# Attention scores in native float32 in the two row halves of TensorE, in a fused attention and MLP kernel

## The chip, the cores and the metric

The kernel runs on one core of a Trainium2 chip, in one launch. The metric is the device time of that launch in microseconds (us); the number given for a kernel is the median of several executions. A profile is one execution recorded by the hardware profiler; its span goes from the first to the last instruction of the program.

## The reference, cut to what matters

```python
# batch 4, 12 heads, 448 positions, 64 numbers per head, all float32
def _attn_ref(q, k, v, w_pre, w_post):
    scores = scale * np.matmul(q, k.transpose(0, 1, 3, 2))
    scores = np.einsum('bhij,hg->bgij', scores, w_pre)      # heads are mixed
    scores = scores - np.max(scores, axis=-1, keepdims=True)
    attn = np.exp(scores)
    attn = attn / (np.sum(attn, axis=-1, keepdims=True) + 1e-09)
    attn = np.einsum('bhij,hg->bgij', attn, w_post)         # and mixed again
    return np.matmul(attn, v)

def _moe_ref(x, w1, w2, w3, w_out):
    return ((x @ w1) * (x @ w2) @ w3) @ w_out

def _moe2_ref(x, w_in, w_out):
    h = np.maximum(x @ w_in, 0.0)
    return h * h @ w_out
# reference = _moe2_ref(_moe_ref(heads of _attn_ref side by side))
```

The weights of the two MLPs arrive as 64-bit words and are narrowed to float32 on the chip. The product w3 @ w_out is formed once at the start and used in place of the two.

## The kernel before, in words

**Precision.** Most products are made of "fp32r" parts: a float32 operand is split into a high part (a rounded copy) and a low part (the rest), and a product is two or three matmuls over these parts. Two products of attention are in native float32 instead: the mixing of the heads before the softmax (`premix`, L380) and the product with v (`pv`, L478). A native float32 matmul stands in the trace as two weight loads and two matmuls.

**Stages.** The program has three. First the product w3 @ w_out (`Prod34`, L119 to L224), in two halves: weights are loaded, joined from their words by VectorE (L93, L95, L97), rounded to the high part by ScalarE (`high`, L111), and the low part is formed by GpSimd (`rest`, L115). In `half1` (L211) the first loop has eight pieces c of 12 matmuls each; ahead of each piece `stage` (L149) issues the preparation of later pieces, and behind it `between(c)` calls `prologue(8 + c)` (L796). Behind this loop stand four blocks of 24 matmuls. Then attention, in 16 chunks n of 120 or 88 query rows (four per batch). Then the two MLPs (`Moe`), about 830 us.

**A chunk of attention.** `scores` (L347) makes the 448 scores of one head for all rows of the chunk. Here a low part is carried along in the contraction: k lies twice, in partitions 0 to 63 and 64 to 127, once as its high and once as its low part (`high_k` L307, `low_k` L315), and q as high and low tiles (`high_q` L330, `low_q` L338); so one head is two fp32r matmuls over 128 partitions and 448 columns:

```python
for i, t in enumerate((self.qh[n, g4], self.ql[n, g4])):
    nc.tensor.matmul(
        sc[:ic], t[:, hh * ic : hh * ic + ic], self.kt[b, h // 2][:, h % 2], start=(i == 0), stop=(i == 1)
    )
```

The result lies in a PSUM tile `sc` of one bank, with two buffers. `evac` (L363) copies it to SBUF with ScalarE, one head at a time. When all 12 heads of a chunk are there, `regroup` (L368) moves blocks of 10 rows by 12 heads to 120 partitions by DMA, so that `premix` can mix heads. From there each block g goes through rowmax (VectorE, L386), `expo` (ScalarE, L394), the normalisation split into fp16 high and low parts (`p_hi` L419, `p_lo` L426), `tmix` (12 fp16 matmuls, L436) and its copy out of PSUM (`p2_evac`, L442: ScalarE where g is a multiple of 4, else VectorE). When a chunk is complete, `pv` multiplies by v. It works on two heads at a time, whose results go to partitions 0 to 63 and 64 to 127 of a PSUM tile, so each matmul uses 64 of TensorE's columns: two column halves.

**Order.** `attention_step(g)` (L549) issues one step for each of 180 blocks. `ORDER` (L536) sets what stands behind what on each engine: on TensorE `pv`, `premix`, `scores`, `tmix`; on ScalarE `evac` (of the step before), `p_hi`, `p2_act`, `pv_out`, `expo`. `LAG` says how many steps behind a block each part runs. `attention_plan` (L510) spreads the 12 heads of chunk n over the steps of the chunk before, and sets when q and k are loaded and split. The first chunk, n = 0, has its own list, `PRO` (L504): at which i of `prologue(i)` its loads, splits, scores and copies are issued, that is behind which piece of the w3 @ w_out product; i = 8 to 15 belong to the eight pieces of the first loop of `half1`, 16 to 19 to its four blocks. Every engine works through its own instructions in the order of issue.

Of the kernel before, what the change touches and what calls it, by code (L numbers as in the profile page):

```python
# [20 lines left out]
IC = 120  # L21
# [13 lines left out]
def fused_kernel(ctx, tc, q, k, v, w_pre, w_post, w1, w2, w3t, wo, win, wo2, eye, out):  # L35
# [83 lines left out]
    class Prod34:  # L119
# [61 lines left out]
        def half0(self, ps, between):  # L181
            acc = {(m, h): ps.tile([128, HC], F, name=f"p34_{m}_{h}") for m in range(4) for h in range(2)}
            for s in range(self.n0):
                self.stage(s)
                c, todo = self.seq[s][1], self.seq[s][5]
                for m, h in todo:
                    self.product(acc[m, h], m, h, (c,))
                if todo and todo[0][1]:
                    between(c)
            for m in range(4):  # L190
                if m > 1:
                    self.stage(self.n0 - 2 + m)
                o = f32(self.spare.tile([128, 2, S], R, tag="kt", name=f"o34_{m}", bufs=8))
                o = o.rearrange("p e j -> p (e j)")[:, :DM]
                nc.scalar.activation(o[:, :HC], acc[m, 0], AF.Copy)
                nc.vector.tensor_copy(o[:, HC:], acc[m, 1])
                nc.scalar.dma_start(
                    w34d[:, :, m].rearrange("n p c -> p n c"), o.rearrange("p (n c) -> p n c", c=128)
                )

        def store(self, m, h, acc):
            if m % 2 == 0:
                self.o = self.spare.tile([128, 3, 2, 128], F, tag="kraw", name=f"o34_{m}_{h}", bufs=2)
# [38 lines left out]
    class Attention:  # L242
        def __init__(self, const, ka, ps):
            self.const, self.ka, self.ps, self.sc = const, ka, ps, {}
            self.done = set()
            self.kt, self.kraw, self.qraw, self.qh, self.ql = {}, {}, {}, {}, {}
# [12 lines left out]


        def setup_load(self):
            nc.vector.memset(self.ones, 1.0)
            for x in self.phl:
                for t in x:
                    nc.vector.memset(t[:, S:], 0.0)
# [13 lines left out]
        def setup_post(self):  # L279
            kw, kab = (self.ka.tile([120, 12, 10], F, tag="qraw", name=x, bufs=2) for x in ("kw", "kab"))  # L280
# [17 lines left out]

        def load_k(self, b, r):
            if b == 0 and r in (2, 3):  # L300
                raw = f32(self.ka.tile([128, 2, S], R, tag="kt", name=f"kraw{b}_{r}", bufs=8))
            else:
                raw = self.ka.tile([128, 2, S], F, tag="kraw", name=f"kraw{b}_{r}", bufs=2)
            nc.sync.dma_start(raw, k[b, :, 2 * r : 2 * r + 2])
            self.kraw[b, r] = raw

        def high_k(self, b, r):  # L307
            t = self.ka.tile([128, 2, S], R, tag="kt", name=f"kt{b}_{r}", bufs=8)
            if b:
                nc.vector.tensor_copy(t, self.kraw[b, r])  # L310
            else:
                nc.scalar.activation(t, self.kraw[b, r], AF.Copy)
            self.kt[b, r] = t

        def low_k(self, b, r):  # L315
            raw, t = self.kraw.pop((b, r)), self.kt[b, r]
            for e in range(2):
                eng = nc.gpsimd if b else nc.vector
                eng.tensor_tensor(t[64:128, e], raw[64:128, e], f32(t[64:128, e]), ALU.subtract)  # L319
            self.done.add(("k", b, r))  # L320

        def load_q(self, n, g4):
            b, c = divmod(n, 4)
            i0, ic, _ = CHUNKS[c]
            o = 12 * i0 + 4 * g4 * ic
            raw = self.ka.tile([128, 4 * IC], F, tag="qraw", name=f"qraw{n}_{g4}", bufs=2)
            nc.sync.dma_start(raw[:, : 4 * ic], q[b, :, o : o + 4 * ic])
            self.qraw[n, g4] = raw[:, : 4 * ic]

        def high_q(self, n, g4):  # L330
            th = self.ka.tile([128, 4 * IC], R, tag="qh", name=f"qh{n}_{g4}", bufs=3)
            th = self.qh[n, g4] = th[:, : 4 * CHUNKS[n % 4][1]]
            if n:
                nc.vector.tensor_copy(th, self.qraw[n, g4])
            else:
                nc.scalar.activation(th, self.qraw[n, g4], AF.Copy)

        def low_q(self, n, g4):  # L338
            tl = self.ka.tile([128, 4 * IC], R, tag="ql", name=f"ql{n}_{g4}", bufs=3)
            tl = self.ql[n, g4] = tl[:, : 4 * CHUNKS[n % 4][1]]  # L340
            nc.gpsimd.tensor_tensor(tl, self.qraw.pop((n, g4)), f32(self.qh[n, g4]), ALU.subtract)

        def split_q(self, n, g4):
            self.high_q(n, g4)
            self.low_q(n, g4)

        def scores(self, n, h):  # L347
            b, c = divmod(n, 4)
            ic = CHUNKS[c][1]
            assert ("k", b, h // 2) in self.done  # L350
            if h == 0:
# [15 lines left out]

        def regroup(self, g):  # L368
            n, r, nr, o, cnt = blocks[g]
            assert all(("s", n, h) in self.done for h in range(NH))  # L370
# [83 lines left out]
        def p2_act(self, g):  # L454
            if g % 4 == 0:
                self.p2_evac(g, 0)

        def p2_dve(self, g):
            if g % 4:
# [34 lines left out]
    def spread(lo, hi, items):  # L494
# [3 lines left out]
    AT = {"sc": 1, "lq": 6, "hq": 3, "pv": 5, "k": -9, "ks": 4, "v": -6}  # L498
# [6 lines left out]
        "load_q": (2, 4, 9), "split_q": (5, 8, 13), "load_k": (7, 7, 8, 8, 8, 8), "high_k": (8, 9, 9, 12, 12, 12),  # L505
        "low_k": (9, 10, 12, 13, 13, 13), "scores": (10, 11, 12, 13, 15, 14), "evac": (10, 11, 13, 14, 15, 14),
# [3 lines left out]
    def attention_plan():  # L510
# [5 lines left out]
        for n in range(16):  # L516
            b = n // 4
            if n:
                for t, h in spread(first[n - 1] - RG + AT["sc"], first[n] - RG - 1, range(NH)):
                    add(t, "scores", n, h)  # L520
                    if h % 4 == 0:
                        add(t - AT["lq"], "load_q", n, h // 4)
                        add(t - AT["hq"], "high_q", n, h // 4)
            for t, x in spread(first[n + 1] + AT["pv"], first[n + 2] + AT["pv"], range(NH // 2)):
                add(t, "pv", n, x)
        for b in range(1, B):
            for r in range(NH // 2):
                t = first[4 * b - 2] + AT["k"] + AT["ks"] * r
                add(t - 3, "load_k", b, r)
                add(t, "high_k", b, r)  # L530
# [8 lines left out]
        ("rowmax", "p_lo", "high_q", "norm_recip", "p2_dve", "high_k"),  # L539
        ("norm_add", "low_q", "low_k"),  # L540
# [6 lines left out]
    AFTER = {"pv_out": "pv", "low_q": "high_q", "low_k": "high_k"}  # L547
# [238 lines left out]
    with tc.manual_schedule(), ExitStack() as base:  # L786
# [9 lines left out]
        def prologue(i):  # L796
# [5 lines left out]
            for kind in ("load_k", "load_q"):  # L802
                for x in at(kind):
                    getattr(A, kind)(0, x)
            for x in at("evac"):
                if PRO["scores"][x] < i:
                    A.evac(0, 2 * x)
                    A.evac(0, 2 * x + 1)
            for kind in ("low_k", "high_k", "split_q"):
                for x in at(kind):  # L810
                    getattr(A, kind)(0, x)
            for x in at("scores"):
                for h in (2 * x, 2 * x + 1):
                    A.scores(0, h)
                    if PRO["evac"][x] == i:
                        A.evac(0, h)
# [19 lines left out]
        for g in step:  # L836
            attention_step(A, g, ev)
            if g == closed:
# [3 lines left out]
                heads = (x for i in range(2) for x in M.early(  # L842
                    i, lambda i: ps.tile([128, TB], F, tag="sc", name=f"e{i}", bufs=2)
                ))
# [65 lines left out]
```

## Time and profile before

| | |
|---|---|
| time, median of 3 runs | 1403.97 us (1403.86 to 1404.88) |
| time of the profiled execution | 1406.93 us |
| its span, first to last instruction | 1405.1 us |
| TensorE (PE) busy | 1360.5 us, 97% of the span |
| VectorE (DVE), ScalarE (ACT), GpSimd (POOL) busy | 919.4, 714.0, 413.5 us |
| mean granted TensorE clock | 0.99 |

How to read it: the trace has one row per instruction. PE is the matmul side of TensorE, PEld its weight loads. A busy share is an average over stages with different limits, so it is read stage by stage. The ends of matmul rows are modelled, so neighbouring rows overlap; how long a group of matmuls holds the engine is better read from the chain of waits, in which each piece ends where the next begins.

### The profile page before, as it was taken

The page shows a single profiled execution, that of the slowest core. Times are in us where ns is not written, and L with a number is a line of the kernel's source. Part 1 is how long each engine was busy: PE and PEld are TensorE (multiplying, and loading weights), DVE is VectorE, ACT ScalarE, POOL GpSimd, SP SyncE. Part 2 cuts the span into 40 slices and gives each one's busy share as a digit, 9 for nine tenths or more (in the row PEclk, how much of TensorE's full clock was granted, in tenths as well). Part 3 has the DMA queues.
Part 4 walks back from the last instruction along what each step waited for, and adds up shares of the span by engine and source line. Part 5 has one row for each costly group of instructions (what it writes and reads, how often), then busy time and mean ns, then how long its engine had stood idle before and what let it go on. Part 6 is the DMA issues. An engine that isn't in the chain of part 4 may idle for free.

```text
span 1405.1 us, 24056 instructions
## 1 busy us (share of the span) xinstructions
PE 1360.5 (97%) x8858; PEld 1141.8 (81%) x8858; DVE 919.4 (65%) x1561; ACT 714.0 (51%) x1529; POOL 413.5 (29%) x424
## 2 busy tenths in 40 slices
PE   6779999999999998999999999999999999999998
PEld 5767666667667666899999999999999999999998
DVE  8963887886887779655217944985555128935962
ACT  4455887877777877434224533543343224533430
POOL 4531351351242113222222222233222222322231
PEclk9889999999999999999999999999999999999999
DMA  7754455454545335434123342455343123432341
GB/s 216 228 187 159 157 167 163 158 177 150 169 165 169 119 128 157 139 102 113 54 69 101 124 120 73 122 176 175 115 115 91 59 78 96 131 115 79 117 145 54
DMA packets 95514, 183.77 MB, mean 131 GB/s; under 512 B 20581, under 2 KB 62053, under 8 KB 94949
## 3 DMA queue, kind: packets, MB, share of 16 engines
q1 hardware_dynamic: 89861, 178.82, 41.2%
q10 hardware_dynamic: 5536, 3.42, 0.8%
q8 instruction: 70, 1.15, 0.4%
q14 instruction: 47, 0.39, 0.1%
HBM read 129.52 MB, written 14.16 MB: 102 GB/s over the span
## 4 chain that ended last, share of the span: by engine, by line
PE 89%; DVE 5%; ACT 2%; issue 2%; DMA 1%; POOL 1%; DVEq 0%; ACTq 0%; POOLq 0%
PE l L54 50%; PE sp L380 10%; PE y L54 8%; PE tp L436 7%; PE pv L478 6%; PE sc L358 5%; PE q L54 2%; DVE pl L426 1%; DVE f L93 1%; DVE f L95 1%; DVE f L97 1%; PE p L54 1%; DVE p L451 1%; PE e L54 1%; ACT ph L419 1%
## 5 line engine op out<-in xcount | busy, mean ns | idle before, releaser
L115 POOL TENSOR_TENSOR wl<-f,wh 128x384 fp32r<-128x384 f32 (+1 forms) x176 | 195.6, 1115 | 508.5 <-ACT wh L111 492.8
L93 DVE TENSOR_SCALAR f<-y 128x384 int32<-128x384 int32 (+2 forms) x209 | 146.9, 703 | 88.2 <-POOL wl L115 83.3
L426 DVE SCALAR_TENSOR_TENSOR pl<-p,sm,ph 120x448 f16<-120x448 f32 x180 | 138.9, 772 | 77.0 <-ACT ph L419 76.3
L380 PE MATMUL sp<-r,kpre 120*120 120x448 f32 x360 | 178.2, 577 | 1.2 <-ACT p L394 0.8
L436 PEld LDWEIGHTS <-ph 120*128 120x128 f16 (+1 forms) x1440 | 105.5, 98 | 52.6 <-issue 52.6
L97 DVE SCALAR_TENSOR_TENSOR f<-raw,f 128x384 int32<-128x384 int32 (+2 forms) x209 | 140.4, 672 | 6.1
L95 DVE SCALAR_TENSOR_TENSOR f<-y,f 128x384 int32<-128x384 int32 (+2 forms) x209 | 140.3, 672 | 6.1
L54 PE MATMUL l<-blh,wh 128*128 128x448 f32 x384 | 141.1, 368 | 0.0
L54 PE MATMUL l<-bhh,wl 128*128 128x448 f32 x384 | 141.1, 368 | 0.0
L54 PE MATMUL l<-bhh,wh 128*128 128x448 f32 x384 | 141.1, 368 | 0.0
L111 ACT ACTIVATE wh<-f 128x384 fp32r<-128x384 f32 (+1 forms) x176 | 96.5, 549 | 86.5 <-DVE f L97 80.9
L365 ACT ACTIVATE s<-sc 120x448 f32<-120x448 f32 (+1 forms) x192 | 99.2, 543 | 76.4 <-PE sc L358 73.0
L436 PE MATMUL tp<-kwh,ph 120*128 120x120 f16 x720 | 125.7, 219 | 1.1 <-DVE p L451 1.1
L394 ACT ACTIVATE p<-sp,nm 120x448 f32<-120x448 f32 x180 | 114.2, 635 | 23.4 <-DVE nm L386 21.9
L386 DVE TENSOR_REDUCE nm<-sp 120x1 f32<-120x448 f32 x180 | 110.6, 615 | 21.0 <-PE sp L380 19.8
L358 PE MATMUL sc<-kt,qh 128*120 128x448 f32 (+1 forms) x192 | 119.5, 622 | 5.0 <-DVE kt L319 4.6
L436 PE MATMUL tp<-kwh,pl 120*128 120x120 f16 x720 | 124.1, 216 | 0.0
L436 PE MATMUL tp<-kwl,ph 120*128 120x120 f16 x720 | 124.0, 216 | 0.0
L81 ACT ACTIVATE y<-raw 128x384 f32<-128x384 f32 (+2 forms) x209 | 120.6, 577 | 5.9 <-DMA raw<-w3t 3.8
L419 ACT ACTIVATE ph<-p,sm 120x448 f16<-120x448 f32 x180 | 119.9, 666 | 5.8 <-DVE sm L414 4.6
L478 PE MATMUL pv<-p,v 112*64 112x120 f32 (+1 forms) x1536 | 94.6, 266 | 6.5 <-DVE p L451 6.2
L409 POOL TENSOR_SCALAR sm<-sm 120x2 f32<-120x2 f32 (+3 forms) x94 | 25.9, 276 | 254.4 <-ACT p L394 226.5
(122 smaller groups left out, 3155.5 us busy)
## 6 DMA issues: line engine op xcount, KB each, us to landing
r<-s SPq DMA_DIRECT2D x172, 210.0 KB
raw<-w SPq DMA_DIRECT2D x64, 384.0 KB
raw<-win SPq DMA_DIRECT2D x64, 384.0 KB
raw<-wo SPq DMA_DIRECT2D x48, 512.0 KB
kraw<-k SPq DMA_DIRECT2D x24, 448.0 KB
qraw<-q SPq DMA_DIRECT2D x36, 240.0 KB
raw<-w3t SPq DMA_DIRECT2D x15, 512.0 KB
raw<-wo SPq DMA_DIRECT2D x16, 384.0 KB
```

The costliest lines, as they stand in the source:

```text
L54: nc.tensor.matmul(acc, w, x, start=(first and i == 0 and j == 0), stop=(last and i == n - 1 and j == 2))
L81: nc.scalar.activation(y, self.raw[i][:, :, 1].bitcast(F), AF.Copy, scale=2.0**-112)
L93: nc.vector.tensor_scalar(fi, yi, 3, 0x7FFFFFFF, ALU.logical_shift_left, ALU.bitwise_and)
L95: nc.vector.scalar_tensor_tensor(fi, yi, -0x80000000, fi, ALU.bitwise_and, ALU.bitwise_or)
L97: nc.vector.scalar_tensor_tensor(fi, raw[:, :, 0], 29, fi, ALU.logical_shift_right, ALU.bitwise_or)
L115: nc.gpsimd.tensor_tensor(self.out[i][1], self.ft.pop(i), f32(self.out[i][0]), ALU.subtract)
L358: nc.tensor.matmul(sc[:ic], t[:, hh * ic : hh * ic + ic], self.kt[b, h // 2][:, h % 2], start=(i == 0), stop=(i == 1))
L380: nc.tensor.matmul(t[:kk], self.kpre[:kk, :kk], self.rt.pop(g)[:kk], start=True, stop=True)
L419: nc.scalar.activation(self.phl[g % NP][0][:kk, :S], self.pt[g][:kk], AF.Copy, scale=self.sm[g // 2][:kk, g % 2 : g % 2 + 1])
L426: nc.vector.scalar_tensor_tensor(l, self.pt.pop(g)[:kk], self.sm[g // 2][:kk, g % 2 : g % 2 + 1], h, ALU.mult, ALU.subtract)
L436: nc.tensor.matmul(t[:, j, :, :cnt], p[:kk, j * JP : j * JP + 128], w[:kk, :, :cnt], start=(i == 0), stop=(i == 2))
L478: nc.tensor.matmul(t[64 * e : 64 * e + 64], self.v[b][:, j, g], self.p2[n][:, j, g, :ic], start=(j == 0), stop=(j == JC - 1),)
```

## The change

The scores become native float32 matmuls over 64 partitions. k and q lie with the even head of a pair in partitions 0 to 63 and the odd head in 64 to 127, as they are in memory; nothing is split, so `high_k`, `low_k`, `high_q`, `low_q` go. A pair of heads x is four matmuls of 224 columns, alternating between the two halves of TensorE's rows, each head into a PSUM bank of its own; the tile `sc` now has two banks and one buffer. One ScalarE copy takes a pair of heads. q is loaded once per chunk, k once per pair of heads and batch. The first chunk's loads, scores and copies get new places. ScalarE's share of `p2_evac` goes from every fourth block to every eighth. A few small tiles change their buffers, and the zeroing of 16 columns of six tiles moves from VectorE to GpSimd.

```diff
         def load_k(self, b, r):
+            t = self.kt[b, r] = self.ka.tile([128, S], F, tag="kt", name=f"kt{b}_{r}", bufs=10)
+            nc.sync.dma_start(t, k[b, :, r])
...
+        def load_q(self, n):
             b, c = divmod(n, 4)
             i0, ic, _ = CHUNKS[c]
+            t = self.ka.tile([128, 6 * IC], F, tag="q", name=f"q{n}", bufs=2)
+            self.qt[n] = t[:, : 6 * ic].rearrange("p (r i) -> p r i", i=ic)
+            nc.sync.dma_start(t[:, : 6 * ic], q[b, :, 6 * i0 : 6 * (i0 + ic)])
...
-            sc = self.ps.tile([IC, S], F, tag="sc", name=f"sc{n}_{h}", bufs=2)
-            g4, hh = divmod(h, 4)
-            for i, t in enumerate((self.qh[n, g4], self.ql[n, g4])):
-                nc.tensor.matmul(
-                    sc[:ic], t[:, hh * ic : hh * ic + ic], self.kt[b, h // 2][:, h % 2], start=(i == 0), stop=(i == 1)
-                )
-            self.sc[n, h] = sc
-
-        def evac(self, n, h):
+            sc = self.sc[n, x] = self.ps.tile([IC, 2, 512], F, tag="sc", name=f"sc{n}_{x}", bufs=1)
+            qt, kt = self.qt[n][:, x], self.kt[b, x]
+            for o in (0, S // 2):
+                w = slice(o, o + S // 2)
+                for e in range(2):
+                    h = slice(64 * e, 64 * e + 64)
+                    nc.tensor.matmul(sc[:ic, e, w], qt[h], kt[h, w], start=True, stop=True)
+
+        def evac(self, n, x):
             ic = CHUNKS[n % 4][1]
-            nc.scalar.activation(self.st[n][:ic, h], self.sc.pop((n, h))[:ic], AF.Copy)
-            self.done.add(("s", n, h))
+            nc.scalar.activation(self.st[n][:ic, 2 * x : 2 * x + 2], self.sc.pop((n, x))[:ic, :, :S], AF.Copy)
+            self.done.add(("s", n, x))
...
         def p2_act(self, g):
-            if g % 4 == 0:
+            if g % 8 == 0:
                 self.p2_evac(g, 0)
...
     PRO = {
-        "load_q": (2, 4, 9), "split_q": (5, 8, 13), "load_k": (7, 7, 8, 8, 8, 8), "high_k": (8, 9, 9, 12, 12, 12),
-        "low_k": (9, 10, 12, 13, 13, 13), "scores": (10, 11, 12, 13, 15, 14), "evac": (10, 11, 13, 14, 15, 14),
+        "load_q": (3,), "load_k": (4, 4, 5, 5, 6, 6), "scores": (9, 10, 11, 12, 13, 14), "evac": (10, 11, 12, 13, 14, 15),
...
             if n:
-                for t, h in spread(first[n - 1] - RG + AT["sc"], first[n] - RG - 1, range(NH)):
-                    add(t, "scores", n, h)
-                    if h % 4 == 0:
-                        add(t - AT["lq"], "load_q", n, h // 4)
-                        add(t - AT["hq"], "high_q", n, h // 4)
+                for t, x in spread(first[n - 1] - RG + AT["sc"], first[n] - RG - 1, range(NH // 2)):
+                    add(t, "scores", n, x)
+                add(first[n - 1] - RG + AT["sc"] - AT["lq"], "load_q", n)
```

## Rows read from the trace of the kernel before

**Rows 1.** Windows by stage: us, busy us (instructions) of each engine, clock, DMA

```profile
0.00:65.00 65.00, 45.31 (x192) 40.76 (x192) 59.80 (x91) 30.26 (x57) 34.32 (x31) 0.89 0.72 214
65.00:104.00 39.00, 28.00 (x124) 24.93 (x124) 29.24 (x46) 20.69 (x37) 15.25 (x11) 0.82 0.64 202
104.00:157.00 53.00, 50.34 (x336) 38.90 (x334) 27.98 (x54) 34.87 (x83) 9.76 (x15) 1.00 0.51 169
157.00:530.00 373.00, 371.20 (x3739) 258.34 (x3740) 295.64 (x556) 293.18 (x679) 110.28 (x154) 1.00 0.47 156
530.00:575.00 45.00, 40.69 (x478) 30.94 (x477) 39.84 (x67) 30.43 (x67) 18.56 (x18) 1.00 0.56 160
575.00:1405.00 830.00, 824.95 (x3996) 747.95 (x3994) 466.91 (x751) 304.53 (x610) 225.34 (x197) 1.00 0.36 106
```

**Rows 2.** Chain of waits, 157 to 530 us: its share by line

```profile
by line: PE sp L380 35.2%; PE tp L436 25.2%; PE pv L478 20.2%; PE sc L358 16.9%; DVE pl L426 0.9%; ACT ph L419 0.5%; DVE p L451 0.5%; issue 0.4%; ACT s L365 0.3%; DVE sm L414 0.1%; ACT p L449 0.0%
```

**Rows 3.** Waits of PE, 157 to 530 us: total us, times, longest

```profile
PE pv L478 <- DVE p L451: 2.8, 3, 1.3
```

**Rows 4.** Groups by form, 157 to 530 us: count | busy us, mean ns | idle, releaser

```profile
L358 PE MATMUL sc<-kt,qh 128*120 128x448 f32 x109 | 68.5, 629 | 0.0
...
L358 PE MATMUL sc<-kt,qh 128*88 128x448 f32 x48 | 31.6, 658 | 0.0
...
L365 ACT ACTIVATE s<-sc 120x448 f32<-120x448 f32 x109 | 56.4, 545 | 42.4 <-PE sc L358 40.7
...
L451 DVE TENSOR_SCALAR p<-tp,iv 112x480 f32<-112x480 f32 x110 | 77.0, 700 | 0.0
```

**Rows 5.** Chain of waits, 381 to 389 us, in order: start, us, what

```profile
382.66 0.63 PE tp L436 x12
383.29 0.97 PE pv L478 x16
384.26 0.94 PE sp L380 x2
...
385.83 0.80 PE sp L380 x2
386.63 0.82 PE sc L358 x4
```

**Rows 6.** Timeline of PE, 402.9 to 403.05 us: start, us, what

```profile
402.94 0.32 PE L478 MATMUL pv<-p,v 112*64 112x120 f32 x2
```

**Rows 7.** Groups by form, 77 to 157 us, ScalarE

```profile
L312 ACT ACTIVATE kt<-kraw 128x896 fp32r<-128x896 f32 x5 | 4.4, 943 | 0.0
```

**Rows 8.** Timeline of PE, 72.5 to 84.7 us: idle and releaser in brackets

```profile
77.21 0.73 PE L358 MATMUL sc<-kt,qh 128*120 128x448 f32 x1 [4.15 <-DVE kt L319]
```

**Rows 9.** Chain of waits, 64 to 105 us

```profile
82.47 0.63 ACT w3h L111
...
87.47 2.63 ACT kt L312 x3
...
91.53 1.20 POOL ql L341
...
93.03 0.78 PE pc L287 x2
...
101.27 2.08 PE q L54 x12
```

**Rows 10.** Windows, 77 to 104 us: 0.53 and 0.54 are the granted clock

```profile
77.00:84.00 7.00, 6.32 (x18) 5.10 (x18) 6.91 (x8) 4.20 (x7) 5.34 (x4) 0.53 0.47 140
...
93.00:97.50 4.50, 4.47 (x15) 4.47 (x16) 3.44 (x12) 0.00 (x0) 0.00 (x0) 0.54 0.64 191
```

**Rows 11.** Timeline of DVE, 74 to 93 us

```profile
76.53 2.20 DVE L319 TENSOR_TENSOR kt<-kraw,kt 64x448 fp32r<-64x448 f32 x2
...
81.76 0.68 DVE L97 SCALAR_TENSOR_TENSOR f<-raw,f 128x512 int32<-128x512 int32 x1
```

**Rows 12.** Chain of waits, 530 to 575 us

```profile
538.93 1.68 DVE pl L426
```

More of the change, by code (lines that the diff above doesn't have):

```diff
@@ L279, in setup_post @@
         def setup_post(self):
-            kw, kab = (self.ka.tile([120, 12, 10], F, tag="qraw", name=x, bufs=2) for x in ("kw", "kab"))
+            kw, kab = (self.ka.tile([120, 12, 10], F, tag="o34", name=x, bufs=4) for x in ("kw", "kab"))
             nc.vector.tensor_tensor(
@@ L299, in load_k @@
         def load_k(self, b, r):
[L300 to L322, printed above, removed]
+            t = self.kt[b, r] = self.ka.tile([128, S], F, tag="kt", name=f"kt{b}_{r}", bufs=10)
+            nc.sync.dma_start(t, k[b, :, r])
+        def load_q(self, n):
@@ L348, in scores @@
+            nc.sync.dma_start(t[:, : 6 * ic], q[b, :, 6 * i0 : 6 * (i0 + ic)])
+        def scores(self, n, x):
             b, c = divmod(n, 4)
             ic = CHUNKS[c][1]
-            assert ("k", b, h // 2) in self.done
-            if h == 0:
+            if x == 0:
                 self.st[n] = (self.ka if n % 2 == 0 else self.kc).tile(
@@ L354, in scores @@
                 )
-            sc = self.ps.tile([IC, S], F, tag="sc", name=f"sc{n}_{h}", bufs=2)
-            g4, hh = divmod(h, 4)
-            for i, t in enumerate((self.qh[n, g4], self.ql[n, g4])):
-                nc.tensor.matmul(
-                    sc[:ic], t[:, hh * ic : hh * ic + ic], self.kt[b, h // 2][:, h % 2], start=(i == 0), stop=(i == 1)
-                )
-            self.sc[n, h] = sc
-        def evac(self, n, h):
+            sc = self.sc[n, x] = self.ps.tile([IC, 2, 512], F, tag="sc", name=f"sc{n}_{x}", bufs=1)
[6 more added lines that the diff above has]
+        def evac(self, n, x):
             ic = CHUNKS[n % 4][1]
-            nc.scalar.activation(self.st[n][:ic, h], self.sc.pop((n, h))[:ic], AF.Copy)
-            self.done.add(("s", n, h))
+            nc.scalar.activation(self.st[n][:ic, 2 * x : 2 * x + 2], self.sc.pop((n, x))[:ic, :, :S], AF.Copy)
+            self.done.add(("s", n, x))
         def regroup(self, g):
             n, r, nr, o, cnt = blocks[g]
-            assert all(("s", n, h) in self.done for h in range(NH))
+            assert all(("s", n, h) in self.done for h in range(NH // 2))
             t = self.kc.tile([120, S], F, tag="r", name=f"r{g}", bufs=6)
@@ L527, in attention_plan @@
             for r in range(NH // 2):
-                t = first[4 * b - 2] + AT["k"] + AT["ks"] * r
-                add(t - 3, "load_k", b, r)
-                add(t, "high_k", b, r)
+                add(first[4 * b - 2] + AT["k"] + AT["ks"] * r, "load_k", b, r)
         for b in range(B):
@@ L538, in fused_kernel @@
         ("evac", "p_hi", "p2_act", "pv_out", "expo"),
-        ("rowmax", "p_lo", "high_q", "norm_recip", "p2_dve", "high_k"),
-        ("norm_add", "low_q", "low_k"),
+        ("rowmax", "p_lo", "norm_recip", "p2_dve"),
+        ("norm_add",),
     )
@@ L546, in fused_kernel @@
     }
-    AFTER = {"pv_out": "pv", "low_q": "high_q", "low_k": "high_k"}
+    AFTER = {"pv_out": "pv"}
     def attention_step(A, g, ev):
@@ L801, in prologue @@
                 A.setup_pre()
-            for kind in ("load_k", "load_q"):
-                for x in at(kind):
-                    getattr(A, kind)(0, x)
+            for x in at("load_k"):
+                A.load_k(0, x)
+            for x in at("load_q"):
+                A.load_q(x)
             for x in at("evac"):
[L806 to L811, printed above, removed]
+                A.evac(0, x)
             for x in at("scores"):
[L813 to L816, printed above, removed]
+                A.scores(0, x)
             if i == PRO["post"]:
@@ L841, in fused_kernel @@
                 tail = M.tail_plan()
-                heads = (x for i in range(2) for x in M.early(
-                    i, lambda i: ps.tile([128, TB], F, tag="sc", name=f"e{i}", bufs=2)
-                ))
+                pair = ps.tile([128, 2, 512], F, tag="sc", name="e", bufs=1)
+                heads = (x for i in range(2) for x in M.early(i, lambda i: pair[:, i, :TB]))
             u = g - closed - 1
@@ L882 @@
     qt = q.transpose(0, 3, 1, 2)
-    qt = np.concatenate([qt[..., o].reshape(B, D, -1) for o in order], axis=2)
-    kt = k.transpose(0, 3, 1, 2)
+    qt = np.concatenate(
+        [qt[..., o].reshape(B, D, 6, 2, -1).transpose(0, 3, 1, 2, 4).reshape(B, 128, -1) for o in order], axis=2
+    )
+    kt = k.reshape(B, 6, 2, S, D).transpose(0, 2, 4, 1, 3).reshape(B, 128, 6, S)
     def words(w):
@@ L894 @@
     arrays = {
-        "q": np.ascontiguousarray(np.concatenate([qt, qt], axis=1)),
-        "k": np.ascontiguousarray(np.concatenate([kt, kt], axis=1)),
+        "q": np.ascontiguousarray(qt),
+        "k": np.ascontiguousarray(kt),
         "v": np.ascontiguousarray(v.reshape(B, NH, JC, JP, D).transpose(0, 3, 2, 1, 4)),
```

32 lines of the change are left out of this document (6 added, 26 removed).

## The prediction, made before the changed kernel was run

> **What bounds the kernel now.** I read the windows by stage first. In the longest stretch of attention, 157 to 530 us, TensorE is busy for 371.2 of 373 us at the full clock (1.00, the 2.4 GHz level), while VectorE and ScalarE are busy for 295.6 and 293.2 us, under 80% [rows 1]. Busy alone proves little where matmul rows overlap, so the chain of waits comes next: in that stretch 97.5% of it is TensorE, in four lines (premix 35.2, tmix 25.2, pv 20.2, scores 16.9%) [rows 2], and its only wait for another engine is 2.8 us in all [rows 3]. So there, whatever VectorE, ScalarE, GpSimd and the DMA queues save buys nothing, and whatever TensorE needs more is paid in full. From 65 to 104 us TensorE is busy for 28 of 39 us at a mean clock of 0.82: it waits [rows 1]. From 530 to 575 us VectorE, at 39.8 of 45 us, ends last. The 830 us of the MLPs are TensorE's and are not touched. What the change is worth is therefore read from the scores on TensorE, and then from the waits ahead of 104 us.
>
> **TensorE's share, 157 to 530 us.** It holds 109 + 48 = 157 heads, 78 pairs [rows 4]. The scores' part of the chain is 16.9% of 373 us = 63 us, 0.80 us a pair; one stretch of two heads shows 0.82 [rows 2, 5]. I take 0.83, since the tmix behind a score is some hundredths longer.
>
> What a pair will cost has two parts. *Passes.* A native float32 matmul is two passes; the premix has two of 448 columns and takes 0.80 us behind a tmix, so at most 0.40 a pass, and about 0.375 without what it pays to begin [rows 5]. A pair now has four matmuls, so eight passes of 224 columns, 0.19 us each. If the row halves work side by side that is four slots, 0.75 us; if not, 1.5. The nearest rows are those of pv, which does the same with column halves: 16 passes of 120 columns, 0.10 each at this pace, would be 1.6 us one by one, but the whole group takes 0.97 [rows 5], and its first two matmuls are a single merged row of 0.32 us, both begun at once [rows 6]. So I take four slots.
>
> *Boundaries.* The rows of pv also show what it costs to cut the array into halves and join it again. Without pv, tmix is followed by a premix of 0.80; with pv, by 0.97 and then a premix of 0.94 [rows 5]. The pv group thus adds 0.97 + 0.14 = 1.11 us for 0.80 us of passes: 0.31 for the two boundaries and the weights that can't be loaded ahead over them. The scores stand between premix and tmix, both on the whole array, so each pair pays two boundaries too. No row shows a boundary of row halves: bounds are 0 (scores today follow the premix with none to be seen) and 0.31 plus some 0.05 for weights of 120 columns instead of 64. I take 0.31, the row that is nearest in kind. A sentence on what the pages say: the Trainium skill ("TensorEngine Tiling (Array Packing)", Key Properties) states that a change of tiling mode drains the engine; no run here shows it yet for row halves, and by that rule a pair costs the 0.31 or more of boundaries, without it 0.75 alone.
>
> So a pair costs 0.75 + 0.31 = 1.06 instead of 0.83: **+0.23 us, times 78 = +18 us**.
>
> **The other twelve pairs of chunks 1 to 15** lie ahead of 157 us. Five stand between the blocks of the w3 @ w_out product, where TensorE is full (50.3 of 53 us) [rows 1]: +1 us. Seven lie from 130 to 157 us, where ScalarE and VectorE take turns with TensorE; I count half: +1 us.
>
> **The other engines in the steady stretch.** One copy of 896 elements takes about 0.94 us (the k rounding of that width) instead of two of 0.545 [rows 4, 7]; 22 of 45 p2 copies go from ScalarE to VectorE at 0.70 each [rows 4]; the q and k splits leave VectorE and GpSimd. All this is under the cover of TensorE. If that cover went, ScalarE's 293 us and VectorE's 296 would be next, far below 373.
>
> **The new wait.** With one buffer, the scores of a pair wait until the copy of the pair before has ended, and tmix of that step is queued behind them. Where two pairs stand in neighbouring steps, tmix (0.63) and premix (0.80 or more) lie between [rows 5], 1.43 us against a copy of 0.94 and its signals, so it hides; it would be late only where ScalarE is still in an exponential, at the most a few tenths on some pairs (0 to 4 us in all; I take 0).
>
> **Loads.** q goes from three issues per chunk to one, k keeps 24 of half the size; SP's queue is shortened, and nothing in the steady stretch waits for it. In the first chunk the six k loads move ahead of VectorE's w3 pieces, into 0 to 65 us, at a DMA share of 0.72 [rows 1]; they could delay those pieces by 0 to 2 us; I take 0, as removed q work on GpSimd there is of the same size.
>
> **The first chunk.** TensorE now stands idle for 4.15 us until 77.21 for the low part of k [rows 8], again until 93.03 for a small matmul whose VectorE input is queued behind a GpSimd split (ql, 91.53) and ScalarE's rounding of k [rows 9], and behind both it runs at a clock of 0.53 and 0.54, about the lower level, 1.2 GHz [rows 10]. These splits go. But ScalarE works in order, and the copy of the first pair is issued behind `high` of a w3 piece, which waits for VectorE's join, ended at 81.76 + 0.68 = 82.44 [rows 11]. Without the 2.20 us of `low_k` ahead of it, that becomes 80.2; plus 0.63 for `high` and 0.94 for the copy, 81.8. TensorE is through with its first pair and third piece at 73.06 + 1.06 = 74.1, and the second pair must wait for the one buffer: 7.7 us idle, and a slow clock behind it. From 81.8: five pairs (5.3), five pieces of 2.08 [rows 9] (10.4), the small matmul (0.4), and some 3 us lost at the slow clock, give 101 against the 104.2 of today (101.27 + 2.08 + a pair): **-3 us**. Bounds: 0, and -12 if the copy came freely.
>
> **The end.** At 530 to 575 us VectorE is last (p_lo, 1.68 us, is in the chain [rows 12]); two more p2 copies of 0.70 go to it: +1 us.
>
> **Sum.** 18 + 1 + 1 - 3 + 1 = +18 us. The profiled execution took 1406.93 us around its span of 1405.1, some 3 above the median; I add to the median: 1403.97 + 18 = **1422 us**.
>
> **Rivals.**
> 1. *No boundary (faster).* Row halves need neither drain nor reload when TensorE goes from premix to scores and on to tmix; a pair is then 0.75 and some 0.04: -0.04 times 90 = -4 us, with -3 in the first chunk and +1 at the end: **1398**. It decides below some 0.10 us for both boundaries together; break-even is there. For it: scores today follow the premix without a seam. Against it: both sides of pv show one. Chance 0.2.
> 2. *One after the other.* The halves do not overlap, so the change does not do what its layout is for: eight slots, +0.75 us on 90 pairs: 1422 + 68 = **1490**. Against it: pv's rows. Chance 0.07.
> 3. *Strict order.* The second pass of the first head must begin before the first pass of the second: five slots instead of four, +0.19 on 90 pairs: **1439**. The rows of pv speak against it (both matmuls of the first row begin together). The Trainium skill ("TensorE: Matmul & The Clock Gate", Part 3, The mechanism) states that matmuls start and end in program order; the trace of pv does not agree as far as two passes of a matmul go, if these stand next to each other. Chance 0.08.
> 4. *Seams half as dear, and a freer first chunk.* 0.15 for both boundaries (+6 us), -10 at the start: about **1402**, no difference. Chance 0.1.
>
> **How the numbers follow.** My forecast has 0.55; its own range is 1412 (the start gains all it can) to 1430 (copies late, dearer weights). Rivals 1 and 4 have 0.3 and pull the low end to 1395; rival 3 sets the high end at 1439; rival 2 is left out. A difference under 0.2% (2.8 us) can't be told from none. Faster: rival 1 and a little, 0.2. Same: 0.1. Slower: the forecast and rivals 2 and 3, 0.7.
>
> **What would show it.** Right: the chain from 160 to 530 us (then longer by some 18 us) is still TensorE; a scores group of eight passes takes 0.9 to 1.1 us in it and the tmix behind it begins later; the premix is unchanged; ScalarE and VectorE fall well below 80%. In the first chunk, a wait of the second pair for the copy behind `high`. Wrong: groups of 0.75 to 0.8 us (rival 1), 1.5 or more (rival 2), about 1.25 (rival 3); or scores that wait for ScalarE in the steady stretch, which I hold to be covered.

## The result and the profile of the changed kernel

The changed kernel takes 1418.64 us (median of 4 runs, 1416.61 to 1420.26) beside 1403.91 us for the kernel before on the same chip: ratio 1.0103, 95% interval 1.0085 to 1.012, so about 1% slower. The profiled execution took 1416.61 us, with a span of 1414.8 us. The unchanged MLP part takes one of two lengths, 3.3 us apart (last section): the profile of before has the longer one, that of the changed kernel the shorter, so I compare stages ahead of the MLPs, and for small differences the start of the first MLP matmul (tile e).

The windows by stage of the changed kernel (us, busy us and instructions of PE, PEld, DVE, ACT, POOL, then clock, DMA share, GB/s) answer to [rows 1]:

```profile
65.00:104.00 39.00, 30.29 (x170) 26.42 (x170) 20.24 (x32) 15.85 (x25) 9.84 (x7) 0.91 0.46 141
...
157.00:530.00 373.00, 372.20 (x3891) 245.51 (x3888) 258.34 (x498) 269.21 (x558) 14.73 (x77) 1.00 0.38 129
```

In the long stretch the three other engines lost work (VectorE 295.64 to 258.34 us, ScalarE 293.18 to 269.21, GpSimd 110.28 to 14.73), and TensorE stayed full. A part of this is only that the same 373 us now hold less work; over equal work, in the two windows further down, VectorE falls from 251.38 to 229.56 us, ScalarE from 251.55 to 239.82 and GpSimd from 94.30 to 13.20. That is the whole case: the work was taken from engines with time to spare and the engine without any got longer steps.

The chain of waits by line, its piece from 388 us on, and the only wait of TensorE, all within 157 to 530 us of the changed kernel, answer to [rows 2, 3, 5]:

```profile
by line: PE sp L342 33.0%; PE tp L398 25.4%; PE sc L323 19.7%; PE pv L440 18.5%; DVE p L413 1.0%; DVE pl L388 1.0%; DVE nm L348 0.6%; issue 0.5%; ACT ph L381 0.4%; DVE sm L376 0.1%; ACT s L327 0.0%
...
388.64 0.63 PE tp L398 x12
389.27 0.97 PE pv L440 x16
390.24 0.94 PE sp L342 x2
391.18 0.63 PE tp L398 x12
391.81 0.80 PE sp L342 x2
392.61 0.92 PE sc L323 x8
393.54 0.74 PE tp L398 x12
...
PE pv L440 <- DVE p L413: 0.8, 2, 0.4
```

A visit of the scores (the matmuls of one pair, between two other groups) is 0.92 us here, 0.95 where a chunk has 120 rows, and the tmix behind it 0.74 us where it is 0.63 elsewhere: 1.03 to 1.06 us a pair. No line says that the scores wait for their single buffer.

To price it over the same work, take the window from the premix of the 31st block to that of the 161st. Both hold 69 pairs and 130 blocks, with two premix matmuls each. The first line is the kernel before, the second the changed one, in two answers of the windows view:

```profile
187.34:506.74 319.40, 317.79 (x3203) 221.91 (x3201) 251.38 (x476) 251.55 (x584) 94.30 (x133) 1.00 0.48 157
```

```profile
185.54:518.28 332.74, 331.94 (x3478) 219.72 (x3477) 229.56 (x442) 239.82 (x498) 13.20 (x69) 1.00 0.39 130
```

332.74 - 319.40 = +13.34 us, 0.193 us a pair. Up to the premix of the 31st block the changed kernel is 1.80 us ahead (185.54 against 187.34). The first matmul of the MLPs begins at 563.4 us before and at 576.4 after. Of its +12.9, then, -1.8 comes from the beginning, +13.3 from these 69 pairs and +1.4 from what follows, where the rest of the pairs and the tail lie.

In the first chunk the timeline of PE and that of ACT show the wait that the single buffer brought, in place of [rows 8, 11] (idle time and its releaser in brackets), and the chain shows the stretch behind it, in place of [rows 9]:

```profile
77.36 0.63 ACT L111 ACTIVATE w3h<-f 128x512 fp32r<-128x512 f32 x1 [1.35 <-DVE f L97]
79.96 0.63 ACT L111 ACTIVATE w3h<-f 128x512 fp32r<-128x512 f32 x1 [1.98 <-DVE f L97]
80.50 0.90 ACT L327 ACTIVATE s<-sc 120x896 f32<-120x896 f32 x1
...
81.45 1.85 PE L323 MATMUL sc<-kt,q 64*120 64x224 f32 x8 [7.61 <-ACT s L327]
...
83.30 3.51 PE q L54 x12
...
87.76 2.28 PE q L54 x12
...
97.67 6.45 PE q L54 x36
```

ScalarE takes a w3 piece at 77.36, waits 1.98 us for VectorE, takes another at 79.96, and only then copies the first pair at 80.50; TensorE stands for 7.61 us. Behind that the first visit takes 1.85 us instead of 0.95 and the first piece 3.51 instead of 2.28; the granted clock of 72 to 84 us is 0.80, a mix of the two levels. The last two pieces (24 matmuls) begin at 97.67 + 6.45/3 = 99.8 us. In the kernel before they begin 4.3 us later, as its chain shows:

```profile
104.16 4.17 PE q L54 x24
```

### The profile page after: what moved, and what is told of

The parts are those of the page before. It is cut to its first block, busy times and chain, and to the rows that moved or that the text cites. A ratio compares the mean times of both kernels' runs of the same rounds, so it can differ in the third digit from the quotient of the medians.

```text
span 1414.8 us, 24393 instructions
## 1 busy us (share of the span) xinstructions
PE 1369.9 (97%) x9242; PEld 1133.0 (80%) x9242; DVE 881.9 (62%) x1502; ACT 692.8 (49%) x1402; POOL 304.2 (22%) x346
## 4 chain that ended last, share of the span: by engine, by line
PE 90%; DVE 6%; issue 2%; ACT 1%; DMA 0%; DVEq 0%; ACTq 0%
PE l L54 50%; PE sp L342 10%; PE y L54 8%; PE tp L398 7%; PE sc L323 6%; PE pv L440 6%; PE q L54 2%; DVE f L93 1%; DVE f L95 1%; DVE f L97 1%; DVE pl L388 1%; DVE p L413 1%; PE e L54 1%; DVE nm L348 0%; ACT s L327 0%
## 5 line engine op out<-in xcount | busy, mean ns | idle before, releaser
L388 DVE SCALAR_TENSOR_TENSOR pl<-p,sm,ph 120x448 f16<-120x448 f32 x180 | 125.5, 697 | 119.0 <-ACT ph L381 119.0
L398 PEld LDWEIGHTS <-ph 120*128 120x128 f16 (+1 forms) x1440 | 109.2, 98 | 69.3 <-issue 69.3
L327 ACT ACTIVATE s<-sc 120x896 f32<-120x896 f32 (+1 forms) x96 | 88.0, 916 | 92.7 <-PE sc L323 91.6
L323 PEld LDWEIGHTS sc<-kt,q 64*120 64x120 f32 (+1 forms) x768 | 61.3, 173 | 69.8 <-issue 28.1
L371 POOL TENSOR_SCALAR sm<-sm 120x2 f32<-120x2 f32 (+3 forms) x94 | 20.1, 214 | 447.8 <-ACT p L356 447.6
L413 DVE TENSOR_SCALAR p<-tp,iv 112x480 f32<-112x480 f32 (+1 forms) x157 | 110.3, 702 | 0.0
```

The costliest lines, as they stand in the source:

```text
L323: nc.tensor.matmul(sc[:ic, e, w], qt[h], kt[h, w], start=True, stop=True)
L388: nc.vector.scalar_tensor_tensor(l, self.pt.pop(g)[:kk], self.sm[g // 2][:kk, g % 2 : g % 2 + 1], h, ALU.mult, ALU.subtract)
L398: nc.tensor.matmul(t[:, j, :, :cnt], p[:kk, j * JP : j * JP + 128], w[:kk, :, :cnt], start=(i == 0), stop=(i == 2))
L413: nc.vector.tensor_scalar(d, t, self.iv[:JP], None, ALU.mult)
```

## The experiments

All are edits of the changed kernel, but for the two that say otherwise. "The changed kernel" is 1418.6 us.

**One matmul per head.** Half as many matmuls and weight loads, the same columns:

```diff
-            for o in (0, S // 2):
-                w = slice(o, o + S // 2)
-                for e in range(2):
-                    h = slice(64 * e, 64 * e + 64)
-                    nc.tensor.matmul(sc[:ic, e, w], qt[h], kt[h, w], start=True, stop=True)
+            for e in range(2):
+                h = slice(64 * e, 64 * e + 64)
+                nc.tensor.matmul(sc[:ic, e, :S], qt[h], kt[h], start=True, stop=True)
```

> Each head of a pair in one matmul of 448 columns instead of two of 224: the same columns and the same two boundaries per pair, but 4 weight loads and 4 passes instead of 8. Theory (two boundaries of the array per pair cost 0.3 us, the rest is passes): a pair stays at 1.05 us, the kernel within 3 us of the changed one (1418.6). Rival (weight loads between the passes hold TensorE up): four loads fewer at about 0.1 us, up to 0.3 us a pair, -10 to -28 us. Rival (passes begin in strict order, so the second head must wait for the first head's second pass): three slots of 0.375 instead of two, +0.37 us on 96 pairs, +36 us.

1418.13 us (1416.41 to 1419.93), ratio to before 1.0089 (1.0066 to 1.0111): no change. The visit keeps its length in the chain, with four matmuls in place of eight:

```profile
393.05 0.92 PE sc L321 x4
393.97 0.74 PE tp L396 x12
```

The price does not hang on the number of matmuls and weight loads.

**Both heads in one half.**

```diff
-                    h = slice(64 * e, 64 * e + 64)
+                    h = slice(0, 64)
```

> Both heads of a pair use the lower row half (partitions 0 to 63), so nothing can overlap; the odd heads' scores are those of the even heads, and what comes behind takes them as they are. Theory (the halves work side by side, four slots of 0.19 us): eight slots instead of four, +0.75 us on 96 pairs; 90 of them where TensorE is full: +65 to +72 us, a group of eight passes at 1.6 to 1.8 us. Rival (the halves hardly overlap and the seams are small): +0 to +20 us.

1489.59 us (1488.16 to 1492.79), 71 us more than the changed kernel. The chain has the visit, and the timeline of PE, over short windows, has its matmuls and their neighbours (start, us, count at the end; several matmuls that overlap make one row):

```profile
388.85 1.70 PE sc L323 x8
390.55 0.74 PE tp L398 x12
```

```profile
388.31 0.54 PE L342 MATMUL sp<-r,kpre 120*120 120x448 f32 x1
...
388.78 0.45 PE L323 MATMUL sc<-kt,q 64*120 64x224 f32 x1
...
389.07 0.73 PE L323 MATMUL sc<-kt,q 64*120 64x224 f32 x3
...
389.83 0.73 PE L323 MATMUL sc<-kt,q 64*120 64x224 f32 x3
...
390.49 0.23 PE L398 MATMUL tp<-kwh,ph 120*128 120x120 f16 x1
```

So in the changed kernel the halves do work side by side (0.92 to 0.95 against 1.70). The starts also show where a visit loses time. From 389.07 to 389.83 there are four steps of 0.19 us. The other three distances are longer: 0.47 us from the premix's second matmul, which has 448 columns, to the first score, 0.29 from the first score to the second, and 0.28 from the last (389.83 + 2 x 0.19 = 390.21) to tmix.

**No change of layout.** q is laid down once per head, with zeros in the other head's 64 rows, and each head's scores use the whole array:

```diff
-            for o in (0, S // 2):
...
+            for e in range(2):
+                nc.tensor.matmul(sc[:ic, e, :S], self.qt[n][e][:, x], kt, start=True, stop=True)
```

> Here each head's scores run over the whole array, with q's other 64 rows set to zero, so premix, scores and tmix all have one shape and no seam is left; a pair then needs four slots of 448 columns in turn. It is to be set beside the run with both heads in the lower half (1489.6 us), which has the same columns in turn and both seams. Theory (two seams cost 0.3 us a pair beside the slots): 90 pairs x 0.3 = 27 us less than that run, about 1462 us (1458 to 1468); the first slot of the scores begins about 190 to 200 ns behind the premix's second one where it now is 469 ns, and the group of the scores stands in the chain at about 1.5 us a pair. Rival (the 0.3 us belongs to the native passes themselves, their two weight loads, not to the change of shape): as that run, 1485 to 1492 us, and the distance from the premix to the scores stays near 470 ns.

1462.65 us (1461.23 to 1463.92): 27 us less than the run before it, though both take the same columns one behind another. Chain and timeline show why:

```profile
390.63 1.51 PE sc L324 x4
392.14 0.63 PE tp L399 x12
```

```profile
390.09 0.54 PE L343 MATMUL sp<-r,kpre 120*120 120x448 f32 x1
...
390.47 0.92 PE L324 MATMUL sc<-kt,q 128*120 128x448 f32 x2
```

The first score follows the premix after 0.38 us, not 0.47 (the 190 to 200 ns expected would fit a matmul of 224 columns; the premix's has 448), and tmix is back at 0.63. Visit and tmix together: 1.70 + 0.74 = 2.44 with the change of layout, 1.51 + 0.63 = 2.14 without, so 0.30 us a pair, and 90 pairs at 0.30 are the 27 us. So the price belongs to the change between the whole array and its halves. Of the three longer distances, the weight loads explain the one behind the first score. The first line is from the run with both heads in one half, the second from this one:

```profile
388.78 0.18 PEld L323 LDWEIGHTS sc<-kt,q 64*120 64x120 f32 x1 [0.66 <-issue]
```

```profile
390.10 0.18 PEld L324 LDWEIGHTS sc<-kt,q 128*120 128x120 f32 x1 [0.19 <-issue]
```

Without a change of layout the weights of the first score start to load at 390.10, 0.37 us ahead of its matmul at 390.47. With one they start only at 388.78, together with the matmul, and the second score follows after 0.29 instead of 0.19: the 0.10 goes with weights that were not loaded ahead. It is 0.26 with the 88 weight columns of a shorter chunk (392.54 to 392.80 us in the changed kernel). The other two parts, 0.09 us each, stand on entering and on leaving.

The Trainium skill ("TensorEngine Tiling (Array Packing)", Key Properties) states that a change of tiling mode drains the engine; these runs agree, in that matmul and weight load both begin later, and give it its size.

**Two visits per pair.** The two 224-column parts of a pair are put on both sides of tmix, which doubles the changes of layout and leaves the columns alone:

```diff
-        ("pv", "premix", "scores", "tmix"),
+        ("pv", "premix", "scores", "tmix", "scores2"),
```

> The same eight passes of a pair in two visits, the first half of the columns ahead of tmix, the second half behind it: two boundaries more per pair, nothing else. Theory (boundaries cost 0.3 us per visit, of which a part is saved where the second visit stands beside pv, which has a boundary there anyhow): +0.15 to +0.3 us on 90 pairs, +14 to +27 us. Rival (no price on boundaries, the pair is slow for another reason): within 3 us of 1418.6.

1448.42 us (1447.98 to 1451.18), 30 us more, a little above what was expected. In the chain:

```profile
392.04 0.57 PE sc L326 x4
392.62 0.74 PE tp L404 x12
393.35 0.57 PE sc L326 x4
393.92 0.94 PE sp L348 x2
```

Two visits of 0.57, a tmix 0.11 longer and a premix 0.14 longer make 1.39 us against 1.05, +0.34 us. This is a pair whose second visit stands ahead of a premix. Where it meets pv, the chain reads:

```profile
446.52 0.57 PE sc L326 x4
447.10 0.74 PE tp L404 x12
447.83 0.57 PE sc L326 x4
448.40 0.97 PE pv L446 x16
```

The changed kernel has 0.95 + 0.74 + 0.97 there, so this pair pays 0.19 us: a part is saved beside pv, as the theory said. Over the same blocks as above (69 pairs, 40 of them beside pv) the run is 24.95 us longer, and 40 x 0.19 + 29 x 0.34 gives 17.5 of them. The other 7 us go with waits: the four lines of TensorE hold 85% of the chain from 157 to 530 us, where they hold 97% in the changed kernel. That these waits come from the pair being complete later is likely, not shown.

**Scores beside pv, first way.** pv moves behind the premix, so that a step that has both runs pv and scores one behind the other:

```diff
-        ("pv", "premix", "scores", "tmix"),
+        ("premix", "pv", "scores", "tmix"),
```

> Order on TensorE premix, pv, scores, tmix instead of pv, premix, scores, tmix. In steps that have both pv and scores (about half) the array goes from column halves straight to row halves, three boundaries instead of four. Theory: 0.15 us less in some 45 steps, -5 to -8 us. Rival (going between two kinds of halves costs as much as two boundaries, or boundaries are not the price): within 3 us of 1418.6.

1416.56 us (1416.03 to 1416.96): 2 us less in the medians, where 5 to 8 were expected, and only 0.3 at the first MLP matmul (576.1 against 576.4 us). The waits of TensorE from 157 to 530 us show the reason, the premix at the head of the step, which now comes before ScalarE has released its buffer:

```profile
PE sp L342 <- ACT p L356: 4.4, 10, 0.9
```

**Scores beside pv, second way.** The scores move in front of the premix, so that nothing comes earlier than it did:

```diff
-        ("pv", "premix", "scores", "tmix"),
+        ("pv", "scores", "premix", "tmix"),
```

> One edit to the changed kernel: in every step TensorE now takes the scores ahead of the premix, so that in a step that has both they stand directly behind pv, which also works on parts of the array. Theory (what costs is each change between the whole array and its parts, and the run with pv moved in front of the scores gave its gain back because its premix then headed the step and waited 4.4 us for ScalarE's exponentials): about half of the 90 pairs share pv's seams, 40 x 0.3 = 12 us less, and no such wait comes up, since the premix now stands later than in the changed kernel: 1405 to 1410 us against 1418.6, with the premix's waits for ScalarE under 1.5 us from 157 to 530 us. Rival (the seam is not shared between column halves and row halves, or the later premix makes the row maximum and the exponential late): 1415 to 1420 us.

1411.66 us (1411.33 to 1414.75), ratio to before 1.0048 (1.0035 to 1.0061): 7 us less in the medians, 5.3 at the first MLP matmul (571.1 against 576.4 us). TensorE has no wait left from 157 to 530 us, and still it is less than 12. The chain:

```profile
388.26 0.92 PE sc L323 x8
389.18 0.94 PE sp L342 x2
...
394.22 0.80 PE sp L342 x2
395.03 0.63 PE tp L398 x12
395.66 0.97 PE pv L440 x16
396.63 0.92 PE sc L323 x8
397.55 0.94 PE sp L342 x2
398.49 0.63 PE tp L398 x12
```

The scores take 0.92 us behind pv as they do behind tmix: going from column halves (pv) to row halves (scores) is a change of layout like the others. A step with both is 0.97 + 0.92 + 0.94 + 0.63 = 3.46 us; in the changed kernel it is 0.97 + 0.94 + 0.92 + 0.74 = 3.57. One change of four is saved, 0.11 us, not two or more. 42 of the steady pairs stand behind pv in the trace: 4.6 us. The other 36 lose a little, 0.92 + 0.94 + 0.63 = 2.49 where the changed kernel has 0.80 + 0.92 + 0.74 = 2.46, some 1 us in all. (The first way saved 0.14 us on a step with both, some 6 us, and the wait of its premix took nearly all of it back: 4.4 us of idle time by the view, and more than that by what is left at the first MLP matmul.) My theory that the two share their seams was half right, and the rival named the reason.

**The first chunk freed.** In the second half of the first product the weight pieces are staged two pieces later, and a pair is copied right behind its scores:

```diff
-                self.stage(self.n0 + 2 + c)
+                if c >= 2:
+                    self.stage(self.n0 + c)
...
-        "scores": (9, 10, 11, 12, 13, 14), "evac": (10, 11, 12, 13, 14, 15),
+        "scores": (9, 10, 11, 12, 13, 14), "evac": (9, 10, 11, 12, 13, 14),
...
-        "post": 12,
+        "post": 14,
```

> Only the first 105 us are changed: in the second half of the first product the pieces of weights are joined two pieces later, and each pair's eviction is issued right behind its scores. Theory (the 7.61 us for which TensorE stood before the second pair of scores was ScalarE's order alone: the eviction stood behind two weight pieces, one of which waited for VectorE): the wait goes, and 6 to 10 us with it, 1408 to 1412 us against 1418, with the steady pairs as they are. Rival (the pieces that now come later are missed by the products, or VectorE's other work takes the place): the wait reappears at the products of this stretch, and the time stays at 1414 to 1420 us. Since the steady stretch costs about 14 us more than before, neither theory lets this kernel go under the kernel before's 1404.

1409.2 us (1405.61 to 1413.04, 12 runs): 9.4 us less in the medians, 10.5 at the first MLP matmul (565.8 against 576.4 us). The stretch from 65 to 104 us, and the chain in it:

```profile
65.00:104.00 39.00, 37.48 (x223) 31.71 (x224) 20.13 (x33) 18.84 (x30) 9.93 (x7) 1.00 0.58 174
```

```profile
74.19 1.02 PE sc L324 x8
75.21 2.27 PE q L54 x12
```

The 7.6 us wait is gone and the clock is 1.00 where it was 0.91, and a piece behind a visit takes 2.27 where the first took 3.51. So the wait came from the place of the copy in ScalarE's order, as the theory said; the two edits, the copy's place and the later pieces, were not tried apart.

**Order and first chunk together.**

> The order of the run above and the edits of the first-chunk run together. Theory (the two costs lie in different stretches and add): 9 us less than the run above, 1396 to 1401 us, which is less than the kernel before's 1404 to 1407, so native scores would win once they neither change the array's shape for themselves nor wait in the first chunk. Rival (as above, the order gives nothing): 1406 to 1411 us.

1403.9 us (1401.6 to 1407.16, 11 runs) beside 1404.91 us: ratio 0.9989 (0.9979 to 0.9999), level with the kernel before. Its MLPs begin at 563.4 us, as before's do. The two gains at that mark (10.5 and 5.3 us) don't quite add: 3 us are missing. The steady stretch has its gain in full: from the 31st block's premix to the 161st's it takes 328.71 us, as with the order alone, against 332.74. What is missing lies on both sides of it. The 31st block's premix comes at 176.7 us, where the first-chunk run has 176.2 and the order alone was 1.2 ahead of the changed kernel; and from the 161st block's premix to the first MLP matmul it takes 58.0 us, as in the changed kernel, where the first-chunk run takes 56.9. Why is open.

**The copies of the second output.** Every fourth p2 copy is on ScalarE again:

```diff
-            if g % 8 == 0:
+            if g % 4 == 0:
...
-            if g % 8:
+            if g % 4:
```

> One edit of the change is undone: every fourth block's second output eviction is back on ScalarE (every eighth in the changed kernel). Theory: it costs something only where VectorE ends the chain, in the some ten blocks behind the last scores (p_hi and p_lo there), so 0 to 1.5 us less than the changed kernel's 1418, and the steady stretch stays as it is. Rival (VectorE's load also slows the steady stretch, by the buffers that it frees late): 3 to 5 us less, with fewer waits between 157 and 530 us.

1418.38 us (1416.87 to 1420.44): nothing to be measured. The MLPs begin at 576.2 instead of 576.4 us, and the steady stretch has 0.6 us of waits instead of 0.8. The copies cost nothing in the stretch and 0.2 us at the end.

**Native scores in the first chunk alone.** This one edits the kernel before: chunk 0 reads raw k and q in row halves, k is split behind it, and the pieces come later as above; the other chunks keep the split operands:

```diff
...
+            for e in range(2):
+                sc = self.sc[0, 2 * x + e] = self.ps.tile([IC, S], F, tag="sc", name=f"sc0_{2 * x + e}", bufs=2)
+                p, o = slice(64 * e, 64 * e + 64), (hh + e) * ic
+                nc.tensor.matmul(sc[:ic], self.qraw[0, g4][p, o : o + ic], self.kraw[0, x][p, e], start=True, stop=True)
...
```

> The kernel before, with native float32 scores in row halves for the first chunk of rows alone, which reads the raw k and q: k is then split later (ScalarE and VectorE, behind that chunk), and the pieces of weights are joined two pieces later as in the run of the first chunk. The 78 pairs behind it keep their split operands and have no seams. Theory (the change's gain lies in the first chunk, where the scores no longer wait for the split of k and q; its loss in the seams): 1404 less 4 to 10 us, 1394 to 1400, with the steady stretch as in the kernel before. Rival (the split is only moved, and its 12 copies on ScalarE of 0.9 us and 12 subtractions on VectorE are missed by the second chunk): 1402 to 1408 us, and a new wait of TensorE for k's split between 95 and 125 us.

1400.01 us (1398.33 to 1405.01, 10 runs) beside 1407.46: ratio 0.9954 (0.994 to 0.9967). It beats both kernels, by 0.3 to 0.6% over the kernel before in the medians. At the first MLP matmul it is 3.6 us ahead (559.8 against 563.4), just under the 4 to 10 of the theory; the rest of the 7.45 between the medians is not shown to come from the edit, since the MLPs behind that mark take either length. How much the later pieces would give to the kernel before without native scores was not tried. Of the waits of TensorE from 60 to 157 us the one for k's split is gone ([rows 8]: 4.15 us); the small matmul's remains:

```profile
PE pc L288 <- DVE kab L286: 4.8, 1, 4.8
```

**That wait removed too.** This edits the run before it. The small matmul's inputs go ahead of k's split on VectorE, the split one step back:

```diff
-        "high_k": (13, 13, 14, 14, 15, 15),
+        "high_k": (14, 14, 14, 15, 15, 15),
```

> The run with native scores in the first chunk alone (1400.0 us), with the small matmul's inputs on VectorE issued ahead of k's split, which is moved back by a step. Theory (TensorE's wait of 4.8 us for that matmul's input is lost time): 3 to 5 us less, 1395 to 1397 us. Rival (the split, now later, is missed by the second chunk's scores, which wait for it instead): 1399 to 1403 us, with a wait of the scores for the low parts of k.

1400.33 us (1397.08 to 1406.07, 12 runs), ratio 0.9964 (0.9951 to 0.9977): no better in the medians, 1.1 us at the first MLP matmul (558.8 against 559.8), where 3 to 5 were expected. The wait is down to 0.4 us and others stand in its place, the longest for q's rounding where I had named k's:

```profile
PE sc L359 <- DVE qh L335: 2.5, 1, 2.5
...
PE pc L288 <- DVE kab L286: 0.4, 1, 0.4
```

## Why the prediction was right, and where its terms were off

**TensorE bounds the steady stretch, and what the others save buys almost nothing.** Shown by the windows above. Almost, because TensorE's wait for VectorE's copy fell from 2.8 us [rows 3] to 0.8; I had valued the relief at nothing, and it is worth 2.

**Four slots, side by side.** Shown: putting both heads in one half cost 71 us, against 68 in my rival 2. Rival 3 (strict order, five slots) fell with the length of the visit, 0.92 to 0.95 us. The Trainium skill ("TensorE: Matmul & The Clock Gate", Part 3, The mechanism) states that matmuls start and end in program order. With one matmul of two passes per head the visit keeps its 0.92 us, so the trace does not agree if the two passes of a head stand next to each other in that order; how they stand, no view shows.

**Boundaries of 0.31 us a pair.** The step that decided the sign, taken from pv as the row nearest in kind. Measured by their absence: 0.30. It divides into some 0.1 us on entering, 0.1 behind the first slot, where the weights were not loaded ahead, and 0.1 on leaving; the prediction had named boundaries and weights, but no split. Rivals 1 and 4 fall with it.

**+0.23 us a pair, +18 us.** Measured 0.193 over the 69 pairs of the same work, some 15 us for 78. The new cost was right (1.03 to 1.06 against 1.06). The old one was set too low: a pair was 0.83 in the stretch that I read, but many steps of the kernel before hold one head alone, and the score there takes 0.41 and the tmix behind it 0.65 rather than 0.63, so a pair split over two steps costs 0.86; and the 2 us of waits above, 0.03 a pair, went with it. This is the mis-sized term.

**One buffer that never waits in the steady stretch, and waits once in the first chunk.** Both as held: 7.7 us idle until 81.8 were forecast, 7.61 until 81.45 measured, by the chain of ScalarE's order that was written down. What it brought there was -4.3 us by 100 us of the run (forecast -3). By the 31st block's premix that is -1.8. Some 18 pairs lie between, the twelve early ones and six of the steady stretch, and they cost 2.5 us; the forecast's terms give 2 + 6 x 0.23 = 3.4.

**The tail, +1 us.** Its reason, the p2 copies on VectorE at the end, is worth 0.2: they are nearly hidden. The stretch behind the 161st block's premix is 1.4 us longer all the same. Its three pairs explain some 0.6; the rest is open, and since the first-chunk run passes the same stretch 1.2 us faster, that it comes near the forecast is luck.

**The total.** +18 was forecast and +12.9 measured ahead of the MLPs, +14.7 between the medians, which hold MLPs of either length. Of the 5 us that the forecast was too high ahead of the MLPs, some 3 are the pairs of the steady stretch (their old cost and its waits) and over 1 is the first chunk.

## What to carry to other kernels

Before a matmul is moved to a part of the array, look in the trace for a place where the kernel already does so and read what its neighbours pay: here pv's rows gave 0.31 us a visit, and 0.30 was measured. A visit must save more than that, so put much work into each and use it where TensorE waits anyway: in the first chunk native scores, together with later weight pieces, gained; in the full stretch they lost. When a buffer is shared by more work, follow the releasing engine's queue in order, since its position there, not its duration, decided the only long wait.

## What was not expected of the hardware

The MLPs, the same instructions in all kernels of this study, take one of two lengths. From the first e matmul to the end of the span it is 841.7 us in the profile of before (1405.1 - 563.4), of the runs with one half, two visits, the whole array and the p2 split, and 841.8 in the run of both edits; it is 838.4 to 838.6 us in the other seven. Compared matmul by matmul in the traces of before and after, the 3.3 us collect evenly in the some 2,300 l matmuls that read x or y, 1.4 ns in each, and not in those that read bh, nor in the y matmuls; no view that I read shows a wait there. The times show it too: the four runs of the changed kernel are 1416.61 and 1417.16, then 1420.12 and 1420.26 us. Its cause stays open.

A change between column halves and row halves costs as much as one between either and the whole array: the scores are 0.92 us behind pv as behind tmix.
